# Batch 1's second FFN product as seven half products for eight, with the copies and sums of the half products placed directly behind them

## The chip, the cores and the metric

One core of a Trainium2 chip runs the whole program. The metric is the device time of one execution in microseconds; several executions are timed and the median is taken. TensorE multiplies matrices into PSUM, VectorE and ScalarE read PSUM and SBUF, GpSimd (POOL) works in SBUF and issues most of the loads, SyncE (SP) issues the stores.

## The reference

Attention with a few global tokens and a local window, then a feed-forward network on its result.

```python
# B, H, Sl, D = 8, 8, 512, 64; Sg = 32; window = 32
s_g = scale * q_g @ concat(k_g, k_l).T;   out_g = softmax(s_g) @ concat(v_g, v_l)
s_l = scale * concat(q_l @ k_g.T, where(|i - j| <= 32, q_l @ k_l.T, -1e9))
out_l = softmax(s_l) @ concat(v_g, v_l)
x = concat(out_g, out_l, axis=2).transpose(0, 2, 1, 3).reshape(4352, 512)
h = x @ w_in                      # 512 -> 2048
g = h * sigmoid(1.702 * h)        # "gelu" below
out = g @ w_out                   # 2048 -> 512, float32
```

## The kernel before

The eight batches go through one after the other, and the work of three stages overlaps: while batch i does its two FFN products, batch i+1 does its attention and batch i+2 has its operands loaded and turned. The global tokens of all batches are collected (`xG`) and go through the FFN at the end. There is no scheduler: each engine gets its instructions in the order in which the Python text issues them, and the framework places semaphore waits where one engine reads or overwrites what another wrote or still reads. `tc.manual_schedule()` says so at the top.

**Attention of one batch** is two quads of four heads, `a` and `c` (class `Wide`, L500). A quad's methods are the steps that the change places anew: `Tk` and `Tq` (L509, L522) turn k and q with VectorE transposes; `kcopy`, `qcopy` and `ext` (L503, L506, L528) copy parts beside them, on VectorE, ScalarE or POOL as told; `S(rnd)` (L548) is one of two rounds of scores on TensorE into four PSUM banks, `X(rnd)` (L568) their exponentials on ScalarE, `M(rnd)` (L573) the mask, a multiplication on VectorE or POOL; `U` and `Gm` (L578, L592) multiply with v on TensorE; `R` (L460) makes the reciprocal of the sums on VectorE, `XL` (L470) scales two tiles of the result into `xL`; `G` (L473), or `keep_og` and `GG` (L606, L609), do the same for the global tokens, `GG` for both quads at once from copies that ScalarE made. S, X and M of round 1 need the banks of round 0 free. `spair()` (L284) gives the four score banks, `pbank()` (L280) one of four others in turn.

**First FFN product**: 16 pieces `fc` of 128 of the 2048 columns, each four matmuls of 128x512 (`h_mm`, L627), then a gelu on ScalarE into `gT` (`h_act`, L650; `h_step`, L654, does both). From batch 3 on (`h_some`, L1197) two pairs of pieces are split: class `HPair` (L689) computes a 2x2 block product with seven half products for eight (Strassen's way with sums). Its `mm(k)` is half product k; products 3 and 4 add into one pair of PSUM banks `x`, in different column halves, 1 and 6 into `y`. `m3` (L715) is a ScalarE copy of product 3 out of `x`, `z` and `zm` (L718, L721) are VectorE sums of it with the next ones, then come `sub` and `add` and two gelus.

**Second FFN product**: in batches 0 and 1 four tiles of 128 rows, each 16 matmuls of 128x512 (`o_mm`, L736), copied out by ScalarE and stored (`o_out`, L854). From batch 2 on class `Pair` (L787) does two such tiles as seven half products of eight matmuls of 128x256, from sums of gT that VectorE makes (`g_sums`, L766) and sums of w_out (`weight_sums`, L753; sums 1 and 2 overwrite two quarters of w_out itself). Again `m3` (L816) copies product 3 from bank `px` to `zz` on ScalarE; `z` reads product 4's half of `px`, `zm` product 1's half of `py`; products 6 and 7 write `py`, 5 and 2 `px`; `evict` is ScalarE's copy of `px`, `sub` and `add` are VectorE's.

**The order around the change.** Batch 0's second product holds batch 1's attention (L954 to L1012). Batch 1's first product follows (L1013 to L1045) with weight sums 0, 3, 4 and the turning of batch 2's operands on VectorE; its second product is `phase_o1` (L1064), `o_mm` pieces between the steps of batch 2's attention. Batch 2's first product is a plain loop (L1287 to L1307). Then `phase_o(i)` (L1107) and `h_some(i)` alternate. In `h_some` the split pair opens with `p.mm(3, 4)`, `p.m3()`; in front of it on ScalarE stand the eviction and `gelu_table()` of `phase_o`'s end. Loads are issued by POOL: `load` (q and k of a batch), `load_v`, `load_g` (global q and k), each waiting until the load eight places ahead has landed.

Of the kernel before, what the change touches and what calls it, by code (L numbers as in the profile page):

```python
# [20 lines left out]
def kernel(  # L21
# [584 lines left out]
    def keep_og(q, ogs):  # L606
        on_act(ogs[:, q.u], q.st["og"][:, : D + 2])
# [60 lines left out]
    def h_weight_sums(g):  # L668
        w11, w12, w21, w22 = w_h[g]
        for t, x, y, op in zip(wh[g], (w11, w21, w11, w21, w12), (w22, w22, w12, w11, w22),  # L670
                               (ALU.add, ALU.add, ALU.add, ALU.subtract, ALU.subtract)):
            nc.vector.tensor_tensor(t, x, y, op)
# [77 lines left out]
    wsum = [wts.tile([128, FC // 2, HM], BF16, name="wsum%d" % k) if k in (0, 3, 4) else (b12, b21)[k - 1]  # L750
            for k in range(5)]

    def weight_sums(*ks):  # L753
        for k in ks:
            x, y, op = ((b11, b22, ALU.add), (b12, b22, ALU.subtract), (b21, b11, ALU.subtract),
                        (b11, b12, ALU.add), (b21, b22, ALU.add))[k]
            nc.vector.tensor_tensor(wsum[k], x, y, op)

    sums = {}

# [182 lines left out]
    for fc in range(4, FC):  # L943
        h_step(0, fc)
        if fc == 4:
            h_weight_sums(1)
        if fc == 12:
            h_weight_sums(2)
            h_weight_sums(4)

    def osteps(i, *sts):
        for tci, f4 in sts:
            o_mm(i, 4 * tci + f4)
# [10 lines left out]
    a.S(0)  # L964
    a.X(0)
    copy_vg1()
    c.Tk()
    c.Tq()
    c.ext()
    a.M(0)  # L970
    osteps(0, (0, 2), (1, 2))
    o_mm(0, 10, part=(0, 1))
    a.S(1)
# [40 lines left out]
    for kcs in ((0, 1), (2,), (3,)):  # L1014
        for fc in range(4):
            h_mm(1, fc, hps[fc], kcs)
    a.G()
    c.G()
    weight_sums(0, 3, 4)
    nq[2][0].Tk()  # L1020
    nq[2][0].Tq()
    transpose_g(4, 6)
    nq[2][0].ext()
    pt = spair()
    for fc in range(4, 8):
        h_mm(1, fc, bank(pt, (fc - 2) % 4), range(NKC))

    a, c = nq[2]
    for fc in range(FC):
        if fc == 11:  # L1030
            c.Tk(False)
            c.Tq(False)
            c.ext((0, 1, 2))
            c.kcopy(nc.vector.tensor_copy)
            c.ext((3,))
            c.qcopy(nc.vector.tensor_copy)
        if fc < 4:
            h_act(1, fc, hps[fc])
        elif fc in (4, 6):
            f = slice(fc, fc + 2)  # L1040
            gelu(gTs[1][:, f, :], pt[1 - (fc - 4) // 2])
        elif fc >= 8:
            h_step(1, fc)
        if fc == 13:
            a.S(0)  # L1045

    def o_parts(i, *parts):
        for part in parts:
            o_mm(i, part)

    def loads_after(i):
        if i + 2 < B:
            load_v(i + 2)
        if i == 1:
            load_g(8, NQ)
        if i + 3 < B:
            load(i + 3)

    def quads_of(n):
        if n < B and n not in nq:  # L1060
# [3 lines left out]
    def phase_o1():  # L1064
        a, c = nq[2]
        a2, c2 = quads_of(3)
        a2.T()
        transpose_g(6, 8)
        a2.ext()
        a.X(0)  # L1070
        a.M(0)
        loads_after(1)
        o_parts(1, 0, 1, 2, 3, 4)
        a.S(1)
        a.X(1)
        a.M(1)
        o_parts(1, 5, 6, 7)
        c.S(0)
        c.X(0)
        a.UG()  # L1080
        a.R()
        c.M(0)
        o_parts(1, 8)
        c.S(1)
        c.X(1)
        a.XL(0)
        a.XL(1)
        a.G()
        c.M(1)
        o_parts(1, 9, 10, 11)  # L1090
        a2.S(0)
        a2.X(0)
        c.UG()
        loads_after(2)
        c.R()
        a2.M(0)
        c.XL(0)
        c.XL(1)
        o_parts(1, 12)
        a2.S(1)  # L1100
        a2.X(1)
        gelu_table()
        c.G()
        a2.M(1)
        o_parts(1, 13, 14, 15)

    def phase_o(i):  # L1107
        b = i + 1
        a, c = nq[b]
        a2, c2 = quads_of(b + 1)  # L1110
        p0, p1 = Pair(i, 0), Pair(i, 1)
        ogs = att.tile([128, 2, D + 2], F32, name="ogs", bufs=1)
        late = a2 and i > 2
        exp_table()
        a.UG()
        c.S(0)
        a.R()
        g_sums(i, 7, 8, (0,))
        a.XL(0)
        wide = 2 < i < B - 1  # L1120
        g_sums(i, 7, 8, (1,) if wide else (1, 2))
        a.XL(1)
        g_sums(i, 7, 8, (3,))
        p0.mm(3, 4, 1)
        c.X(0)
        p0.m3()
        p0.z()
        if wide:
            g_sums(i, 4, 8, (2,))
# [12 lines left out]
        p0.mm(5, 2)  # L1142
        p0.sub()
        p0.evict()
        p0.mm(7)
        p0.add()
        p0.store()
        if a2:
            c.UG()
            c.R()  # L1150
            keep_og(c, ogs)
            if i + 3 < B:
                load_v(i + 3, chunks=(0, 1))
            a2.S(0)
            a2.X(0)
            a2.M(0, nc.gpsimd)
            if i + 3 < B:
                load_v(i + 3, chunks=(2, 3, 4))
        else:
            pt = spair()  # L1160
            c.U(0, bank(pt, 0))
            c.U(1, bank(pt, 2))
            c.U(2, bank(pt, 3))
            c.Gm(bank(pt, 1))
            c.R()
            keep_og(c, ogs)
        c.XL(0)
        if a2:
            c.XL(1)
            GG(b, ogs)  # L1170
        p1.mm(3, 4)
        p1.m3()
        p1.z()
        if c2:
            c2.Tk(False)
        else:
            c.XL(1)
# [12 lines left out]
        gelu_table()  # L1190
        p1.mm(7)
        p1.add()
        if a2:
            a2.M(1, nc.gpsimd if i + 3 < B else nc.vector)
        p1.store()

    def h_some(i):  # L1197
# [7 lines left out]
        gs = (1, 2) if c else (1,)  # L1205
        fcs = iter([fc for fc in range(2, 8) if fc // 2 not in gs])
        p = HPair(i, *gs)
        p.mm(3, 4)
        p.m3()
        for fc in range(2):  # L1210
            h_act(i, fc, hps[fc])
        if c:
# [40 lines left out]
            h_step(i, 15)  # L1253
            return
        p = HPair(i, 4)
        p.mm(3, 4)
        p.m3()
        g_sums(i, 0, 2, (0, 1))
        p.z()
        p.mm(1, 6)  # L1260
# [20 lines left out]
        g_sums(i, 4, 6, (3,))  # L1281
        g_sums(i, 6, 8, (3,))

    for i in range(1, B):
        if i > 2:
            h_some(i)
        elif i > 1:  # L1287
            for fc in range(FC):
                h_step(i, fc)
                if i == 2 and fc == 0:  # L1290
                    weight_sums(1, 2)
                if i + 1 < B:
                    c = nq[i + 1][1]
                    if fc == 1:
                        c.Tk()
                        c.Tq()
                        c.ext((3,))
                    if fc in (3, 5, 7):
                        c.ext(((3, 5, 7).index(fc),), on_act)
                    if fc == 9 and i + 2 < B:  # L1300
                        a2 = quads_of(i + 2)[0]
                        a2.T()
                        transpose_g(2 * i + 4, 2 * i + 6)
                        a2.ext()
                if fc in (4, 8, 12):
                    g_sums(i, fc // 2 - 2, fc // 2)
                if fc == 13:  # L1307
                    g_sums(i, 6, 7)
        if i == 1:
            phase_o1()  # L1310
        elif i + 1 < B:
            phase_o(i)

    scores.close()
# [85 lines left out]
```

## Time and profile before

| | |
|---|---|
| median of 3 runs | 284.52 us (284.43 to 284.99) |
| the profiled execution | 284.57 us, its span 282.9 us |
| TensorE clock granted | 1.0 throughout |
| VectorE / ScalarE / POOL busy | 226.6 / 187.1 / 109.9 us |

The stages around the change, from the windows of the profile (us of the span; busy time with instructions in brackets for TensorE, its weight loads, VectorE, ScalarE and POOL; then the granted clock, the DMA share and GB/s). In order: batch 1's first product, its second (`phase_o1`), batch 2's first, its second (`phase_o(2)`).

```profile
51.00:66.00 15.00, 14.74 (x93) 6.76 (x90) 12.34 (x32) 8.49 (x15) 10.30 (x16) 1.00 1.16 189
66.00:85.90 19.90, 19.74 (x366) 10.67 (x368) 15.26 (x32) 15.72 (x18) 14.51 (x21) 1.00 1.57 158
85.90:99.63 13.73, 13.62 (x62) 6.07 (x63) 12.71 (x31) 10.60 (x21) 3.95 (x6) 1.00 1.32 161
99.63:117.44 17.81, 17.76 (x394) 15.23 (x395) 16.66 (x37) 11.11 (x16) 7.29 (x7) 1.00 0.34 47
```

A busy TensorE row counts matmuls that overlap in a pipeline; the number of matmuls and the step from one to the next say more than the share.

### The profile page before, as it was taken

The numbers are of one execution on the slowest core, as the hardware profiler recorded it, in microseconds if no ns is written. First come the engines' busy times: TensorE is split into PE (matmuls) and PEld (weight loads), VectorE is DVE, ScalarE is ACT, GpSimd is POOL, SyncE is SP. The second block draws the span as 40 slices with busy tenths as digits, with TensorE's granted clock in tenths as the row PEclk, the third lists the DMA queues.
The fourth block names the chain that finished last, engine by engine and source line by source line (L and its number), as shares of the span: only waits on it lengthen the run. The fifth ranks groups of instructions, "written<-read, shape, count | busy, mean of one in ns | idle before, by whom it ended". The sixth has DMA issues, their size and how long they took to land.

```text
span 282.9 us, 9001 instructions
## 1 busy us (share of the span) xinstructions
PE 274.3 (97%) x3764; PEld 184.5 (65%) x3787; DVE 226.6 (80%) x490; ACT 187.1 (66%) x319; POOL 109.9 (39%) x157
## 2 busy tenths in 40 slices
PE   6899999999999999999999999999999999999994
PEld 6554445544554478756886488757876589558884
DVE  6687367985689898989998899899997898586452
ACT  4848667577778785579756994779648961873331
POOL 8973551764946004970099106930070000000001
PEclk9999999999999999999999999999999999999999
DMA  7999996899999903994089807920023003300223
GB/s 207 162 196 211 204 156 85 142 220 141 166 166 191 154 3 45 110 158 84 6 115 132 148 5 85 103 58 2 22 59 74 2 2 77 74 3 0 59 53 114
DMA packets 59352, 28.24 MB, mean 100 GB/s; under 512 B 47472, under 2 KB 49776, under 8 KB 59312
## 3 DMA queue, kind: packets, MB, share of 16 engines
q0 software_dynamic: 51760, 17.83, 55.7%
q1 hardware_dynamic: 7120, 9.18, 11.9%
q8 instruction: 29, 0.48, 0.7%
q10 hardware_dynamic: 432, 0.66, 0.7%
q14 instruction: 11, 0.09, 0.1%
HBM read 36.31 MB, written 8.91 MB: 160 GB/s over the span
## 4 chain that ended last, share of the span: by engine, by line
PE 93%; DVE 2%; DMA 2%; ACT 1%; issue 1%; SPq 0%; DVEq 0%
PE hp L629 32%; PE px L812 13%; PE op L743 10%; PE py L812 9%; PE x L812 6%; PE s L560 6%; PE s L711 5%; PE ov L586 5%; PE s L629 2%; DMA early<-in_q_l_dram 2%; DVE xL L471 1%; PE og L597 1%; PE s L357 1%; ACT e L388 1%; PE s L340 1%
## 5 line engine op out<-in xcount | busy, mean ns | idle before, releaser
L629 PE MATMUL hp<-xL,w_in_sb 128*128 128x512 bf16 x385 | 88.7, 379 | 0.9 <-DVE xL L471 0.2
L629 PEld LDWEIGHTS <-w_in_sb 128*128 128x128 bf16 x496 | 48.2, 98 | 48.1 <-issue 0.4
L634 ACT ACTIVATE gT<-hp 128x512 bf16<-128x512 f32 x100 | 57.1, 601 | 13.4 <-PE hp L629 13.0
L571 ACT ACTIVATE e<-s 128x1016 bf16<-128x1016 f32 (+1 forms) x56 | 53.2, 1003 | 17.8 <-PE s L560 17.8
L98 POOL DMA_DIRECT2D v<-in_v_l_dram x40 | 31.1, 779 | 62.8 <-PE og L597 52.6
L812 PEld LDWEIGHTS <-gs 128*128 128x128 bf16 x480 | 46.2, 98 | 6.4
L785 DVE TENSOR_TENSOR gs<-gT 128x256 bf16<-128x256 bf16 (+2 forms) x75 | 28.1, 405 | 4.7 <-ACT gT L634 4.7
L576 POOL TENSOR_TENSOR e<-e,mask 128x1760 bf16<-128x1760 bf16 (+1 forms) x7 | 23.1, 3303 | 19.8 <-ACT e L571 19.7
L812 PE MATMUL py<-wsum,gs 128*128 128x256 bf16 x240 | 30.3, 273 | 0.0
L743 PE MATMUL op<-w_out_sb,gT 128*128 128x512 bf16 x122 | 28.8, 380 | 0.5 <-issue 0.3
L845 POOL DMA_DIRECT2D out_dram<-ob x2 | 1.2, 597 | 65.8 <-ACT ob L113 65.6
L576 DVE TENSOR_TENSOR e<-e,mask 128x1712 bf16<-128x1712 bf16 (+1 forms) x21 | 22.1, 1052 | 2.7 <-ACT e L571 2.4
L512 DVE STREAM_TRANSPOSE kT<-rk 128x512 f32<-128x512 f32 x14 | 14.6, 1041 | 12.0 <-DMA rk<-in_k_l_dram 12.0
L743 PEld LDWEIGHTS <-gT 128*128 128x128 bf16 x128 | 11.8, 98 | 13.9
L812 PEld LDWEIGHTS <-gT 128*128 128x128 bf16 x192 | 18.0, 98 | 2.9
L812 PE MATMUL px<-w_out_sb,gT 128*128 128x256 bf16 x160 | 19.2, 273 | 0.0
L812 PE MATMUL px<-w_out_sb,gs 128*128 128x256 bf16 x160 | 19.1, 273 | 0.0
L471 DVE TENSOR_TENSOR xL<-ov,rs 128x512 bf16<-128x512 f32 x27 | 17.9, 685 | 0.7 <-PE ov L438 0.3
L113 ACT ACTIVATE ob<-px 128x512 f32<-128x512 f32 x10 | 6.0, 598 | 17.9 <-DVE zz L834 17.9
L560 PEld LDWEIGHTS <-kT 32*128 32x128 bf16 x672 | 12.5, 93 | 6.8 <-issue 4.9
L634 ACT ACTIVATE gT<-s 128x1024 bf16<-128x1024 f32 (+1 forms) x10 | 9.3, 938 | 11.5 <-DVE ob L725 7.0
L782 DVE TENSOR_TENSOR gs<-gT 128x1024 bf16<-128x1024 bf16 (+3 forms) x21 | 15.9, 760 | 0.0
(181 smaller groups left out, 452.6 us busy)
## 6 DMA issues: line engine op xcount, KB each, us to landing
out_dram<-ob SPq DMA_DIRECT2D x128, 64.0 KB, 2.4
rq<-in_q_l_dram POOLq DMA_DIRECT2D x5, 512.0 KB, 7.3
rk<-in_k_l_dram POOLq DMA_DIRECT2D x5, 512.0 KB, 8.5
v<-in_v_l_dram POOLq DMA_DIRECT2D x24, 96.0 KB, 4.1
w_in_sb<-in_moe_w_in_dram POOLq DMA_DIRECT2D x8, 256.0 KB, 8.9
w_out_sb<-in_moe_w_out_dram POOLq DMA_DIRECT2D x4, 512.0 KB, 10.6
rk<-in_k_l_dram POOLq DMA_DIRECT2D x5, 256.0 KB, 7.9
rq<-in_q_l_dram POOLq DMA_DIRECT2D x5, 256.0 KB, 7.3
```

The lines of the kernel that those rows point to most:

```text
L98: nc.gpsimd.dma_start(out=vt[0:n, hs, c, :D], in_=vs[FIRST[c] : FIRST[c] + n, hs])
L471: nc.vector.tensor_mul(self.x[:, 2 * self.u + h, :], self.st[1 + h], self.st["rs"])
L512: nc.vector.transpose(flat[:, 0:Sl].rearrange("p (r t) -> p t r", t=16), loaded[self.b][0][:, self.u].bitcast(F32))
L560: nc.tensor.matmul(bank(self.ps, j)[:, at : at + n], lhsT=self.k[p, KEYS[c] : KEYS[c] + 128, e], rhs=qs[p, :, :, e], start=(e == 0), stop= ...
L571: nc.scalar.activation(self.E[rnd][:, 2 * i : 2 * i + 2, :n], self.ps[i][:, :, :n], AF.Exp, scale=scale)
L576: eng.tensor_mul(e, e, mask[:, rnd : rnd + 1, :n].to_broadcast([128, 4, n]))
L629: nc.tensor.matmul(hp[:, : width(i)], lhsT=w_in_c[:, fc // 4, kc, fc % 4 // 2, :, fc % 2], rhs=(xL[i] if i < B else xG)[:, kc, :], start=( ...
L634: nc.scalar.activation(out_, in_, AF.Gelu_apprx_sigmoid)
L743: nc.tensor.matmul(op, lhsT=gTs[i][:, fc, tci * 128 : tci * 128 + 128], rhs=w_out_sb[:, fc, :], start=(first and fc == 4 * f4), stop=(fc = ...
L782: nc.vector.tensor_tensor(sums[i][2][:, g, :n], t[:, g, 0, :n], t[:, g, 1, :n], ALU.add)
L785: nc.vector.tensor_tensor(sums[i][k][:, g, : n // 2], x[:, g], y[:, g], op)
L812: nc.tensor.matmul(out_, lhsT=lv[:, g, tt * 128 : tt * 128 + 128], rhs=rv[:, g, :], start=(g == 0 and k in ((1, 3, 4, 6) if self.apart els ...
```

## The change

Batch 1's second product now goes through `Pair` too, in a new `phase_o1` with its own order of half products, scores and copies. The weight sums are made earlier, 0, 3 and 4 in pieces during batch 0's second product, 1 and 2 during batch 1's first. Batch 1's global rows are kept by ScalarE copies. Batch 2's operand copies of quad a go to ScalarE. Batch 2's first product becomes `h_two`, which holds round 1 of batch 3's scores. In `phase_o(2)` the copies for batch 4 go to ScalarE as they did from `phase_o(3)` on. In `h_some`, in both split pairs, `m3` is issued between half products 3 and 4, where it was issued behind 4.

```diff
-    def weight_sums(*ks):
+    def weight_sums(*ks, g=slice(0, FC // 2)):
...
-            nc.vector.tensor_tensor(wsum[k], x, y, op)
+            nc.vector.tensor_tensor(wsum[k][:, g], x[:, g], y[:, g], op)
...
         if fc == 12:
             h_weight_sums(2)
             h_weight_sums(4)
+    weight_sums(0, 3, 4, g=slice(2, 4))
+    weight_sums(0, 3, 4, g=slice(0, 2))
...
     copy_vg1()
+    weight_sums(0, 3, 4, g=slice(4, 6))
...
     a.M(0)
+    weight_sums(0, 3, 4, g=slice(6, 8))
...
-    a.G()
-    c.G()
-    weight_sums(0, 3, 4)
-    nq[2][0].Tk()
-    nq[2][0].Tq()
-    transpose_g(4, 6)
-    nq[2][0].ext()
+    ogs = att.tile([128, 2, D + 2], F32, name="ogs", bufs=1)
+    keep_og(a, ogs)
+    keep_og(c, ogs)
+    weight_sums(1, 2)
+    GG(1, ogs)
...
+        if fc == 3:
+            g_sums(1, 0, 2)
+            a.Tk(False)
+            a.Tq(False)
+            transpose_g(4, 6)
+        if fc == 6:
+            g_sums(1, 2, 4)
+            c.Tk(False)
+            c.Tq(False)
+            c.kcopy(nc.vector.tensor_copy)
+            c.qcopy(nc.vector.tensor_copy)
+            c.ext()
+        if fc == 8:
+            a.kcopy(on_act)
+        if fc == 9:
+            a.qcopy(on_act)
+        if 10 <= fc < 14:
+            a.ext((fc - 10,), on_act)
         if fc == 13:
-            a.S(0)
+            g_sums(1, 4, 7, (0, 1))
```

The new phase and batch 2's first product, the old bodies left out:

```diff
     def phase_o1():
         a, c = nq[2]
         a2, c2 = quads_of(3)
+        p0, p1 = Pair(1, 0), Pair(1, 1)
+        ogs = att.tile([128, 2, D + 2], F32, name="ogs", bufs=1)
+        load_g(8, NQ)
+        load(4)
+        load_v(3, chunks=(0, 1))
+        g_sums(1, 7, 8, (0, 1))
+        p0.mm(3)
+        p0.m3()
+        p0.mm(4)
+        a.S(0)
         a.X(0)
+        p0.z()
+        g_sums(1, 4, 8, (2, 3))
+        p0.mm(1)
+        p0.zm()
+        p0.mm(6, 5)
         a.S(1)
         a.X(1)
+        a2.Tk(False)
+        a.M(0)
+        p0.mm(2)
+        p0.sub()
+        p0.evict()
+        p0.mm(7)
         a.M(1)
         c.S(0)
         c.X(0)
+        p0.add()
+        p0.store()
+        ov = [pbank("ov"), pbank("ov")]
+        p1.mm(3)
+        p1.m3()
+        a.U(0, ov[0])
+        a.U(1, ov[1])
+        a.U(2)
         a.R()
         c.S(1)
         c.X(1)
+        p1.mm(4)
+        a.Gm()
+        keep_og(a, ogs)
+        a2.kcopy(on_act)
+        c.M(0, nc.gpsimd)
+        load_v(3, chunks=(2, 3, 4))
         a.XL(0)
+        p1.z()
         a.XL(1)
+        p1.mm(1)
+        p1.zm()
+        a2.Tq(False)
+        transpose_g(6, 8)
+        a2.qcopy(on_act)
+        a2.ext(copy=on_act)
         c.M(1)
+        p1.mm(6, 5, 2)
+        p1.sub()
+        p1.evict()
+        p1.mm(7)
+        p1.add()
+        p1.store()
         a2.S(0)
+        ov = [pbank(n) for n in ("ov", "og", "ov", "ov")]
+        c.U(0, ov[0])
+        c.U(1, ov[2])
+        c.U(2, ov[3])
+        c.Gm(ov[1])
+        a2.X(0, (0,))
+        keep_og(c, ogs)
+        a2.X(0, (1,))
         c.R()
-        a2.M(0)
+        a2.M(0, nc.gpsimd)
         c.XL(0)
         c.XL(1)
+        return ogs
+
+    def h_two(ogs):
+        a, c = nq[3]
+        a2 = quads_of(4)[0]
+        pool = nc.gpsimd.tensor_copy
+        gTs[2] = moe.tile([128, FC, TB], BF16, name="gT")
+        hps = [pbank("hp") for _ in range(4)]
+        for fc in (0, 1):
+            h_mm(2, fc, hps[fc], (0, 1))
+        a.S(1)
+        a.X(1)
         gelu_table()
+        for fc in (2, 3):
+            h_mm(2, fc, hps[fc], (0, 1))
+        for kc in (2, 3):
+            for fc in range(4):
+                h_mm(2, fc, hps[fc], (kc,))
+        pt = spair()
+        for fc in range(4, 8):
+            h_mm(2, fc, bank(pt, fc - 4), range(NKC))
+        c.Tk(False)
+        c.Tq(False)
+        c.kcopy(pool)
+        c.qcopy(pool)
+        c.ext((3,), pool)
+        load_v(4)
+        load(5)
+        a2.Tk(False)
+        a2.Tq(False)
+        transpose_g(8, 10)
+        GG(2, ogs)
+        a.M(1)
+        for fc in range(4):
+            h_act(2, fc, hps[fc])
+        g_sums(2, 0, 2)
...
     def phase_o(i):
...
-        late = a2 and i > 2
+        late = a2
...
     def h_some(i):
...
         p = HPair(i, *gs)
-        p.mm(3, 4)
+        p.mm(3)
         p.m3()
+        p.mm(4)
...
         p = HPair(i, 4)
-        p.mm(3, 4)
+        p.mm(3)
         p.m3()
+        p.mm(4)
...
-    for i in range(1, B):
...
+    h_two(phase_o1())
+    phase_o(2)
+    for i in range(3, B):
+        h_some(i)
+        if i + 1 < B:
             phase_o(i)
```

More of the change, by code (lines that the diff above doesn't have):

```diff
@@ L1029 @@
     for fc in range(FC):
[L1030 to L1036, printed above, removed]
         if fc < 4:
@@ L1043 @@
             h_step(1, fc)
-        if fc == 13:
-            a.S(0)
[L1047 to L1057, printed above, removed]
+        if fc == 3:
[16 more added lines that the diff above has]
+            a.ext((fc - 10,), on_act)
+        if fc == 13:
+            g_sums(1, 4, 7, (0, 1))
     def quads_of(n):
@@ L1066, in phase_o1 @@
         a2, c2 = quads_of(3)
-        a2.T()
-        transpose_g(6, 8)
-        a2.ext()
-        a.X(0)
-        a.M(0)
-        loads_after(1)
-        o_parts(1, 0, 1, 2, 3, 4)
+        p0, p1 = Pair(1, 0), Pair(1, 1)
[8 more added lines that the diff above has]
+        a.S(0)
+        a.X(0)
+        p0.z()
+        g_sums(1, 4, 8, (2, 3))
@@ L1074, in phase_o1 @@
+        p0.mm(1)
+        p0.zm()
+        p0.mm(6, 5)
         a.S(1)
         a.X(1)
+        a2.Tk(False)
[4 more added lines that the diff above has]
+        p0.mm(7)
         a.M(1)
-        o_parts(1, 5, 6, 7)
         c.S(0)
         c.X(0)
-        a.UG()
+        p0.add()
[6 more added lines that the diff above has]
+        a.U(2)
         a.R()
-        c.M(0)
@@ L1083, in phase_o1 @@
-        o_parts(1, 8)
         c.S(1)
         c.X(1)
+        p1.mm(4)
[4 more added lines that the diff above has]
+        load_v(3, chunks=(2, 3, 4))
         a.XL(0)
+        p1.z()
         a.XL(1)
-        a.G()
-        c.M(1)
-        o_parts(1, 9, 10, 11)
-        a2.S(0)
-        a2.X(0)
-        c.UG()
-        loads_after(2)
+        p1.mm(1)
[3 more added lines that the diff above has]
+        a2.qcopy(on_act)
@@ L1095, in phase_o1 @@
+        a2.ext(copy=on_act)
+        c.M(1)
+        p1.mm(6, 5, 2)
[4 more added lines that the diff above has]
+        p1.store()
+        a2.S(0)
+        ov = [pbank(n) for n in ("ov", "og", "ov", "ov")]
[6 more added lines that the diff above has]
+        a2.X(0, (1,))
         c.R()
-        a2.M(0)
+        a2.M(0, nc.gpsimd)
         c.XL(0)
         c.XL(1)
-        o_parts(1, 12)
@@ L1100, in phase_o1 @@
-        a2.S(1)
-        a2.X(1)
-        gelu_table()
-        c.G()
-        a2.M(1)
-        o_parts(1, 13, 14, 15)
+        return ogs
[9 more added lines that the diff above has]
+        a.X(1)
+        gelu_table()
+        for fc in (2, 3):
[21 more added lines that the diff above has]
+        g_sums(2, 0, 2)
+        for n in range(2):
+            gelu(gTs[2][:, 4 + 2 * n : 6 + 2 * n, :], pt[n])
+        g_sums(2, 2, 4)
+        for fc in range(8, FC):
+            h_step(2, fc)
+            if fc in (9, 10, 12):
+                c.ext(((9, 10, 12).index(fc),), on_act)
+            if fc == 11:
+                g_sums(2, 4, 6)
+            if fc == 13:
+                g_sums(2, 6, 7)
@@ L1282, in h_some @@
         g_sums(i, 6, 8, (3,))
-    for i in range(1, B):
[L1285 to L1311, printed above, removed]
+    h_two(phase_o1())
[3 more added lines that the diff above has]
+        if i + 1 < B:
             phase_o(i)
```

## The prediction

> **What bounds the kernel now.** I read the page first (busy time, chain), then the waits of TensorE, then the timeline where the changed lines stand. All durations are from the one profiled execution: 284.57 us, of which the span is 282.9 and 1.7 lies around it; the median of the runs is 284.52, so a change of the span is carried over one to one.
>
> ```profile
> span 282.9 us, 9001 instructions
> ...
> PE 274.3 (97%) x3764; PEld 184.5 (65%) x3787; DVE 226.6 (80%) x490; ACT 187.1 (66%) x319; POOL 109.9 (39%) x157
> ...
> PE 93%; DVE 2%; DMA 2%; ACT 1%; issue 1%; SPq 0%; DVEq 0%
> ```
>
> TensorE works 97% of the span and holds 93% of the chain that ended last. Its waits, all longer ones of the whole run (engine and line, what was waited for, us, times, longest):
>
> ```profile
> PE s L357 <- DVE q L316: 1.7, 2, 1.5
> PE w L183 <- POOL ones L159: 1.1, 1, 1.1
> PE s L340 <- ACT e L388: 0.4, 1, 0.4
> PE op L743 <- issue: 0.3, 2, 0.2
> PE s L865 <- issue: 0.2, 1, 0.2
> PE s L629 <- DVE sT L462: 0.2, 1, 0.2
> PE hp L629 <- DVE xL L471: 0.2, 1, 0.2
> ```
>
> The chain has the last of these at 53 us; behind it TensorE never waits noticeably. So a wait put in front of TensorE there has no idle time to go into: it adds its whole length. Work taken off TensorE gains its whole length if its feeders keep up.
>
> The place that decides is the start of a split first product, here batch 3's (start, us, engine, line):
>
> ```profile
> 118.36 0.60 ACT L113 ACTIVATE ob<-px 128x512 f32<-128x512 f32 x1 [1.79 <-DVE zz L834]
> ...
> 118.95 0.60 PE L711 MATMUL s<-sT,w_in_sb 128*128 128x256 bf16 x4
> 118.98 1.28 ACT L634 ACT_TABLE_LOAD   x1
> ...
> 119.38 0.60 PE L711 MATMUL s<-xs,w_in_sb 128*128 128x256 bf16 x4
> ...
> 120.27 0.20 ACT L634 ACTIVATE spot<-spot 128x1 f32<-128x1 f32 x1
> 120.38 0.58 ACT L113 ACTIVATE ob<-s 128x512 f32<-128x512 f32 x1
> ...
> 120.99 0.69 DVE L719 TENSOR_TENSOR ob<-ob,s 128x512 f32<-128x512 f32 x1 [0.91 <-ACT ob L113]
> ```
>
> TensorE does half product 3 (operands sT, w_in) at 118.95 and half product 4 (xs, w_in) at 119.38, right behind it. ScalarE copies product 3 only from 120.38 to 120.96: before that it evicts the last tile of the phase, itself held until 118.36 by VectorE, and loads the gelu table. Today nobody on TensorE waits for that copy.
>
> **The change, part by part.**
>
> (1) Fewer products. Batch 1's second product was 64 matmuls of 512 columns; batch 2's first product, the same 64, takes the chain from 85.89 to 99.70, so 13.81 us. Now it is 2 tiles x 7 half products; the chain gives one (eight matmuls of 256) as 0.87: 14 x 0.87 = 12.2. Gain 1.6.
>
> (2) m3 before mm(4) in the split first products (batches 3 to 7, and a second one in 7). The order in which the changed kernel is built has a wait there that the old one lacks: half product 4's first matmul waits for the ScalarE copy of product 3. It writes other columns, but of the same PSUM bank that the copy reads. ScalarE's own order in front of the copy is unchanged (eviction, table load, a dummy gelu, copy), and what holds the eviction (VectorE's sums L685 and L686 ahead of its L834) is unchanged too. So the wait costs from product 4's start today to the copy's end plus the 0.03 that VectorE needs to start on it (120.99 against 120.96). From the timeline at each place: batch 3: 120.99 - 119.38 = 1.6; batch 4: 152.16 - 150.53 = 1.6; batch 5: 183.23 - 181.62 = 1.6; batch 6: 214.75 - 212.73 = 2.0; batch 7: 243.57 - 242.34 = 1.2, and its second 248.47 - 247.32 = 1.15. Sum 9.2. Queued behind it on TensorE are products 4, 1, 6 and the rest of the first product; ScalarE's gelus and VectorE's sums all become due later, so nothing is gained back. Bounds: no gain, since TensorE has no waiting there to lose, and at least the bare copy, if ScalarE stood ready: 4 x (0.17 end of the matmul, 0.03, 0.58, 0.03) + 2 x 0.6 = 4.4; at most these 9.2 plus 1. I take 9.2, since both ends of each subtraction are rows of the same queues.
>
> The row shows no TensorE wait on another half of a bank, so the trace alone cannot say that the wait must be there; the built order does. The Trainium skill (PSUM — Partial Sum Buffer, PSUM bank collisions raise a hardware error) gives the reason: two engines may not be on the same bank and quadrant together, even at disjoint columns, so semaphores guard by bank. By it the sum is the one here; with a guard by columns it would be the second rival's below.
>
> (3) The same inside batch 1's new phase (starting when its first product ends, about 65.3: 65.99 less the 0.6 of a.S(0), which moves behind it). First tile: mm(4) waits for m3: matmul end 0.17, copy 0.39 (L113 128x256), twice 0.05: 0.65. mm(6) now stands behind zm and waits for it, and VectorE has z 0.33 (L824 at 104.32, the next at 104.65), sums of 2048 elements 1.14 (L782, 1.22 busy) and of 1024 some 0.6, then zm 0.41 (L827) between mm(4)'s end and that point: 0.22 + 2.48 = 2.7 (steps from start to start), while TensorE has only a.S(0) 0.67 and mm(1) 0.97: 1.1 of stall. Second tile: mm(6) behind zm again, VectorE free: 0.17 + 0.41 + 0.07 = 0.65; its mm(4) has U, R and S(1) before it and does not wait. c.S(0) comes only mm(2) and mm(7) (1.85) behind a.S(1) and needs the banks that a.X(1) reads (1.89 plus latency): 0.25; in the old order 2.7 of products stood between. a2.S(1), inside the next first product, needs both halves of X(0), with keep_og between them: 0.45. One more change of matmul shape (0.1, as 1.85 against 2 x 0.87). Sum 3.2. Bounds: 1.3 (the two zm and m3 at a bare 0.4) to 7 (every chain here late by a VectorE transpose, mask and sums, 1.04 + 1.05 + 1.6).
>
> (4) What I cost at nothing, with the cover. Weight sums 0, 3, 4 in twelve pieces of 512 (0.37 each, L785's): six lie in VectorE's 6.5 us of waiting for rk before 32.95 (the POOL queue shows those w_out parts landed by 28.3 and 30.7), three before c.Tk (1.9 idle, part landed by 36.4), three behind a.M(0), which moves a.M(1) to 43.6-44.7, its reader a.U(0) starting at 46.0. Uncovered they are 1.1 a group. Weight sums 1, 2 (2.33) move into the 3.46 that the others leave at 54.9. g_sums of batch 1 (two groups of 1.6, then 0.5 + 0.5 and 0.25 + 0.25), with Tk 1.04, Tq 0.7 and copies, end by my addition at 66.6; mm(1), their first reader, starts at about 68.3, so 1.7 us are spare. c.Tk lies among them and waits for its DMA until 62.19, as today. ScalarE gets six copies (0.3 to 0.54) between gelus of 0.6 in steps of 0.86: gelu 14 ends near 65.2, in time. Evictions turn from four of 0.6 into m3 0.39 and one of 0.6 a tile. On POOL, load_g and load(4) go ahead of load_v(3), then come c.M(0) and a2.M(0) at 3.3 each and three copies: c.M(0) can start at 77.7 and ends at 81, its reader c.U(0) comes at 85; load_v(4), now some 8 us later, is read at 130. SP issues the same 16 stores. In phase_o(2) a2's copies go to ScalarE as in phase_o(3): those two phases last 17.81 and 17.78 today, so nothing.
>
> Sum: -1.6 + 9.2 + 3.2 = 10.8 on 284.57: 295.4, and 295.3 on the median. I forecast 295.3; its own range is 292.5 to 298.
>
> **The rivals.**
>
> A. ScalarE gets to the copy at once, so (2) costs only the bare copies, 4.4: 284.5 - 1.6 + 4.4 + 3.2 = 290.5. For it: in batch 7 the gap is already smaller. Against: the table load of 1.28 starts only behind an eviction that VectorE releases, in every batch at the same distance.
>
> B. The other side: the half products run on without the wait for the copies, and seven for eight is all that is left. Then (2) and the m3 and zm terms of (3) fall away: 284.5 - 1.6 + 0.25 + 0.45 + 0.1 = 283.7, faster. It decides once the waits on copies sum to under 0.8 us over six first products and one phase, that is 0.1 each. For it: the columns are disjoint. Against: the built order names the wait at each place, and one bare copy alone is 0.39.
>
> C. VectorE falls behind in batch 1's new phase. Between 51.0 and 85.9 it is busy 12.34 + 15.26 = 27.6 of 34.9 us. Added are g_sums 6, the two tiles' z, zm, sub, add 2 x 2.2 and weight sums 2.3; gone are weight sums 3.5, two masks to POOL 2.1, and copies of some 2: 32.7 of 34.9. With waits inside, a chain may slip by 3.7 in (3): 284.5 + 14.5 = 299. Against: the spare 1.7 and 0.7 above.
>
> **How the numbers follow.** Forecast 0.74, A 0.10, B 0.06, C 0.10. The range is 290.5 to 298: it takes in A's value and the forecast's own range, and leaves out B and most of C. A measurement of this kernel tells 0.2% (0.6 us) from no change. Faster: B, 0.06. Within 0.2%: 0.01, for cases between B and A. Slower: 0.93.
>
> **What would show it.** In the profile after: TensorE waits at L711 released by ScalarE's L113 copy, six times, 1.1 to 2.0 us each, about 9 in all; at L812 waits on L113 and L827 between 65 and 82; busy TensorE time down by 1.6 while its share falls to about 93%. Batch 2's first product would end near 101, against 99.7 today; from there each batch would be 1.6 longer. If L711 shows no waits, (2) is wrong; if they are near 0.8, A holds; if VectorE is the releaser of long waits between 66 and 90, C.

## The result, and the profile after

| | kernel before | changed kernel |
|---|---|---|
| median of 6 runs each, us | 284.36 (284.06 to 284.99) | 296.34 (296.17 to 296.65) |
| ratio, 95% interval | | 1.0421 [1.0407, 1.0434] |
| profiled run, us | 284.57 | 296.17 |
| its span, us | 282.9 | 294.5 |

The change costs 12 us; 295.3 was predicted. Where it costs them is read first from TensorE's share. The page of the changed kernel, with span, busy time of the engines and the chain that ended last:

```profile
span 294.5 us, 9145 instructions
...
PE 276.2 (94%) x3815; PEld 190.2 (65%) x3835; DVE 231.9 (79%) x494; ACT 191.6 (65%) x339; POOL 117.6 (40%) x162
...
PE 12%; ACT 1%; DVE 0%; issue 0%; ACTq 0%
```

TensorE fell from 97% of the span to 94%: it is idle 18.3 us where it was 8.6. The chain can't be set beside that of before: it is followed back only to 250 us here, so its shares add up to 13%. The waits say more. TensorE's longest waits in the changed kernel (engine, tile and line, what was waited for, us in total, times, longest):

```profile
PE s L711 <- ACT ob L113: 8.7, 6, 1.9
PE py L812 <- DVE zz L827: 1.6, 2, 1.1
PE w L183 <- POOL ones L159: 1.1, 1, 1.1
PE px L812 <- ACT zz L113: 0.5, 1, 0.5
```

The third line stood there before. The other three are new, and they are the three kinds that the prediction named: half product 4 of the split first products behind ScalarE's copy (L711, six times), and in batch 1's phase `mm(6)` behind `zm` (L827) and `mm(4)` behind `m3` (L113). Together they are 10.8 us. The waits in batch 1's phase, each on the first matmul of a half product (start, us; in brackets the idle time before it and what ended it):

```profile
66.29 1.03 PE L812 MATMUL px<-w_out_sb,gT 128*128 128x256 bf16 x8 [0.47 <-ACT zz L113]
...
69.97 1.03 PE L812 MATMUL py<-wsum,gs 128*128 128x256 bf16 x8 [1.09 <-DVE zz L827]
...
80.70 1.03 PE L812 MATMUL py<-wsum,gs 128*128 128x256 bf16 x8 [0.51 <-DVE zz L827]
```

The timeline of the changed kernel at batch 3's first split product, the place that the prediction showed of before (start, us, engine, line, operation; in brackets the idle time before it and its releaser):

```profile
120.40 0.60 ACT L113 ACTIVATE ob<-px 128x512 f32<-128x512 f32 x1 [1.81 <-DVE zz L834]
...
120.97 0.60 PE L711 MATMUL s<-sT,w_in_sb 128*128 128x256 bf16 x4
121.02 1.28 ACT L634 ACT_TABLE_LOAD   x1
...
122.31 0.20 ACT L634 ACTIVATE spot<-spot 128x1 f32<-128x1 f32 x1
122.42 0.58 ACT L113 ACTIVATE ob<-s 128x512 f32<-128x512 f32 x1
...
123.05 0.60 PE L711 MATMUL s<-xs,w_in_sb 128*128 128x256 bf16 x4 [1.49 <-ACT ob L113]
```

ScalarE's row is the one of before, 2.04 us later throughout: eviction, table load, dummy gelu, copy. On TensorE half product 4, which used to start 0.43 behind product 3 (119.38 and 118.95), starts 2.08 behind it (123.05 and 120.97), when the copy is done. That is 1.65 more; 1.6 was predicted for this place.

The whole run can be cut at the first matmul that each batch's attention does with its summed weights (`ov<-e,ones`, L586). In the changed kernel two of these rows read:

```profile
101.64 0.55 PE L586 MATMUL ov<-e,ones 128*32 128x128 bf16 x24
...
134.40 0.55 PE L586 MATMUL ov<-e,ones 128*32 128x128 bf16 x24
```

All of them, as lengths of the stretch from one to the next, in us:

| stretch | before | after | difference | predicted |
|---|---|---|---|---|
| up to batch 1's phase | 46.00 | 45.64 | -0.36 | 0 |
| batch 1's phase and batch 2's first product | 53.63 | 56.00 | +2.37 | +1.6 |
| batch 3's split product in it | 31.10 | 32.76 | +1.66 | +1.6 |
| batch 4's | 31.15 | 32.98 | +1.83 | +1.6 |
| batch 5's | 31.09 | 32.73 | +1.64 | +1.6 |
| batch 6's | 31.11 | 33.14 | +2.03 | +2.0 |
| batch 7's two, to the end of the span | 58.82 | 61.25 | +2.43 | +2.35 |

The last five rows are the copy in front of half product 4: 9.6 against 9.2. The second is batch 1's phase. The first is not the work of the change: TensorE is 0.36 us ahead already at the first matmul of batch 0's first product (17.32 against 17.68), where it has done nothing new yet and has only waited less for q at L357 (0.2 against 1.7 in all). The kernels of the experiments that open as the changed one does take 45.5 to 46.5 us for this stretch, and 47.0 in one execution that was slow throughout, at a lower clock.

### The profile page after: what moved, and what is told of

Read it like the earlier page. It is cut to its first block, busy times and chain, and to the rows that moved or that the text cites. A ratio compares the mean times of both kernels' runs of the same rounds, so it can differ in the third digit from the quotient of the medians.

```text
span 294.5 us, 9145 instructions
## 1 busy us (share of the span) xinstructions
PE 276.2 (94%) x3815; PEld 190.2 (65%) x3835; DVE 231.9 (79%) x494; ACT 191.6 (65%) x339; POOL 117.6 (40%) x162
## 5 line engine op out<-in xcount | busy, mean ns | idle before, releaser
L629 PE MATMUL hp<-xL,w_in_sb 128*128 128x512 bf16 x370 | 85.6, 379 | 1.1 <-DVE xL L471 0.2
L812 PEld LDWEIGHTS <-gs 128*128 128x128 bf16 x560 | 53.9, 98 | 9.5 <-issue 2.0
L576 POOL TENSOR_TENSOR e<-e,mask 128x1760 bf16<-128x1760 bf16 (+1 forms) x9 | 29.8, 3313 | 28.2 <-ACT e L571 28.1
L812 PE MATMUL py<-wsum,gs 128*128 128x256 bf16 x288 | 36.6, 273 | 1.7 <-DVE zz L827 1.6
L785 DVE TENSOR_TENSOR gs<-gT 128x256 bf16<-128x256 bf16 (+3 forms) x86 | 32.7, 410 | 6.5 <-ACT gT L634 6.5
L812 PE MATMUL px<-w_out_sb,gT 128*128 128x256 bf16 x192 | 23.4, 273 | 0.5 <-ACT zz L113 0.5
L812 PEld LDWEIGHTS <-gT 128*128 128x128 bf16 x224 | 20.9, 98 | 4.3 <-issue 0.6
L812 PE MATMUL px<-w_out_sb,gs 128*128 128x256 bf16 x192 | 23.1, 273 | 0.0
L113 ACT ACTIVATE ob<-px 128x512 f32<-128x512 f32 x12 | 7.2, 598 | 18.9 <-DVE zz L834 18.9
L100 POOL DMA_DIRECT2D v<-in_v_g_dram x24 | 14.0, 584 | 2.3 <-DMA rq<-in_q_l_dram 1.7
L560 PE MATMUL s<-q,kT 32*128 32x160 bf16 (+1 forms) x448 | 14.9, 246 | 0.0
```

The source lines that it names most:

```text
L100: nc.gpsimd.dma_start(out=vt[96:128, :, c, :D], in_=vg)
L560: nc.tensor.matmul(bank(self.ps, j)[:, at : at + n], lhsT=self.k[p, KEYS[c] : KEYS[c] + 128, e], rhs=qs[p, :, :, e], start=(e == 0), stop= ...
L576: eng.tensor_mul(e, e, mask[:, rnd : rnd + 1, :n].to_broadcast([128, 4, n]))
L629: nc.tensor.matmul(hp[:, : width(i)], lhsT=w_in_c[:, fc // 4, kc, fc % 4 // 2, :, fc % 2], rhs=(xL[i] if i < B else xG)[:, kc, :], start=( ...
L785: nc.vector.tensor_tensor(sums[i][k][:, g, : n // 2], x[:, g], y[:, g], op)
L812: nc.tensor.matmul(out_, lhsT=lv[:, g, tt * 128 : tt * 128 + 128], rhs=rv[:, g, :], start=(g == 0 and k in ((1, 3, 4, 6) if self.apart els ...
```

## The experiments

The ratios are to the kernel before, timed beside each; its median was 284.35, 284.47 and 284.29 in the three groups. "Kernel 2" is the kernel of experiment 2, and so on.

**1. The copy moved alone** (copy_between_alone). The kernel before, and nothing of the change but step (2), in both places:

```diff
-        p.mm(3, 4)
+        p.mm(3)
         p.m3()
+        p.mm(4)
```

> The kernel before, with only the two lines of the split pairs changed: m3 between half products 3 and 4. Theory W: six waits, 9.2 us by the subtraction of rows, up to 9.6 by the stages: 284.4 + 9.2 to 9.6 = 293.6 to 294.0 us. Rival L: a few us at most, since the rest of the change, which would make the engines late, is missing: 285 to 290.

Measured 293.92 us, ratio 1.0333 [1.0315, 1.0352]: 9.6 us for one step moved in two places, with batch 1's product as it was. TensorE's longest wait in that kernel:

```profile
PE s L711 <- ACT ob L113: 8.4, 6, 1.9
```

The idle time is 8.4 and the time lost 9.6. Most of the rest is the end of the last matmul before each wait, which otherwise overlaps the next one: in the rows above, product 4 starts 1.65 later for 1.49 of idle time, and there are six such places.

**2. The copy moved back** (split_pairs_old_order). The changed kernel with step (2) undone, all else kept.

```diff
-        p.mm(3)
+        p.mm(3, 4)
         p.m3()
-        p.mm(4)
```

> The changed kernel, but in the split first products of batches 3 to 7 half product 4 is issued ahead of the copy m3 again, as before the change. Theory W (each wait of half product 4 for the copy adds its whole length to the path): the stages of batches 2 to 7, which became 9.6 us longer, go back, so 296.3 - 9.6 = 286.7 us, and TensorE has no wait at the half products' line. Rival L (the stages are longer because ScalarE and VectorE do more and are late for other reasons, the wait only shows it): well above, 290 or more. Rival S (batch 1's new phase is the larger loss): above 288.

Measured 293.13 us, 1.0308 [1.0289, 1.0328]: not theory W's 286.7, but where rivals L and S had put it. The L711 waits on L113 were gone, yet only 3.2 us came back. The cut by stretches shows where they stayed: 56.00, then 31.10, **37.72**, 31.10, 31.10 and 58.78. Batch 1's phase has the length that it has in the changed kernel, so it is not S. Of the stretches behind it every one has the length of before (58.78 against 58.82 for the last), but for one that is 6.6 longer. So L's general lateness did not hold either. TensorE's longest waits in this kernel:

```profile
PE px L812 <- DVE zz L824: 2.7, 1, 2.7
PE s L711 <- DVE sT L685: 2.0, 1, 2.0
...
PE s L711 <- DVE ob L719: 0.8, 1, 0.8
```

These three are waits on VectorE, each once and all in the long stretch. VectorE's timeline there, with POOL's:

```profile
146.30 3.88 DVE L613 TENSOR_TENSOR xgg<-ogs,rgg 128x128 bf16<-128x128 f32 x1
146.67 3.34 POOL L576 TENSOR_TENSOR e<-e,mask 128x1760 bf16<-128x1760 bf16 x1
...
152.65 4.80 DVE L685 TENSOR_TENSOR sT<-xL 128x512 bf16<-128x512 bf16 x2
...
153.56 3.27 POOL L576 TENSOR_TENSOR e<-e,mask 128x1712 bf16<-128x1712 bf16 x1
```

L613, 0.29 us in every other phase of this run, takes 3.88 and ends at 150.18, just after POOL's mask multiplication (150.01). What stands behind it on VectorE slides by 3.6, so that the pair of L685, 1.55 before, comes to lie beside POOL's second mask and takes 4.80, to 157.45, where the mask ends at 156.83. That gave a new theory: these VectorE instructions stand until POOL's has ended. Two kernels tested it.

**3. A pause on POOL** (pause_before_mask). Kernel 2 with 0.6 us of useless work added:

```diff
+    pause = consts.tile([128, 4], F32)
...
             a2.X(0)
+            if i == 3:
+                for _ in range(4):
+                    nc.gpsimd.memset(pause, 0.0)
             a2.M(0, nc.gpsimd)
```

> split_pairs_old_order with four tiny memsets of 128x4 on POOL ahead of the first mask multiplication of batch 3's phase (i == 3): no work is moved or taken away, POOL's mask starts some 0.4 us later (0.1 each by the small memsets at the kernel's start). Theory P with a race at the start (line 613 began at 146.30 and POOL's mask is recorded from 146.67, so close together that which of the two goes first decides): the VectorE instruction is through before the mask starts, takes 0.29, and the time is 293.1 - 6.6 = 286.5 to 287. Rival V (order on VectorE or ScalarE): unchanged, 293.1. If 0.4 is too little for the race, 293.1 too, with line 613 still at 3.9.

Measured 286.93 us, 1.0096 [1.0082, 1.0110]: work added to an engine, and 6.2 us gained. VectorE and POOL in that stretch (line numbers behind 635 are higher by 1 here):

```profile
145.94 0.29 DVE L613 TENSOR_TENSOR xgg<-ogs,rgg 128x128 bf16<-128x128 f32 x1
...
146.29 0.60 POOL L1241 MEMSET pause<- 128x4 f32 x4
...
146.85 3.32 POOL L576 TENSOR_TENSOR e<-e,mask 128x1760 bf16<-128x1760 bf16 x1
146.90 1.03 DVE L512 STREAM_TRANSPOSE kT<-rk 128x512 f32<-128x512 f32 x1
...
147.78 0.40 DVE L828 TENSOR_TENSOR zz<-zz,py 128x256 f32<-128x256 f32 x1
...
148.71 2.07 DVE L686 TENSOR_TENSOR sT<-xL 128x512 bf16<-128x512 bf16 x2
```

L613 is through before the mask starts. Under the mask the transpose (one input) and L828 (its second input, py, is in PSUM) keep their durations; the pair sT (two inputs in SBUF) is longer again, by 0.5, and ends 0.6 after the mask. The Trainium skill (SBUF — State Buffer, Who interferes with whom) states that a VectorE instruction with two SBUF inputs contends with a GpSimd instruction that reads SBUF, for ports under an exclusive lock, and that the order of issue decides which of the two is blocked. The trace agrees on the hold: 3.88 for 0.29.

The pair's usual 1.55 is such a hold too. A single sum of this shape takes 0.41 in the same stretch (L685's third, `xs`). In the kernel before, the pair lies under the first mask as well, and ends 0.63 after it (116.80 and 116.17):

```profile
112.83 3.34 POOL L576 TENSOR_TENSOR e<-e,mask 128x1760 bf16<-128x1760 bf16 x1
...
115.25 1.55 DVE L685 TENSOR_TENSOR sT<-xL 128x512 bf16<-128x512 bf16 x2
```

In the stretches of batches 3 to 6, before and after, it ends 0.6 to 0.8 behind that mask every time.

What stays open is why L613 was struck there. In kernel 2 the held L613 is recorded 0.37 ahead of the mask; in batch 3's stretch of the same run it is 0.37 ahead too (114.84 and 115.21), and takes 0.29. The recorded starts don't say which of the two came first.

**4. The mask on VectorE** (mask_on_vector_batch3_phase). Kernel 2 with the first of that stretch's two masks off POOL:

```diff
-            a2.M(0, nc.gpsimd)
+            a2.M(0, nc.vector if i == 3 else nc.gpsimd)
```

> split_pairs_old_order with one instruction moved: in batch 3's phase (i == 3) the first mask multiplication goes from POOL to VectorE. Split_pairs_old_order took 293.13 us, of which one stage has 6.6 more than its neighbours (37.72 against 31.1), with a VectorE multiplication of 3.88 us (0.29 elsewhere) under POOL's mask multiplication. Theory P (that VectorE instruction stands until POOL's mask multiplication beside it has ended, and everything behind it slides): without the POOL instruction beside it, line 613 takes 0.29 again, the stage 31.1 plus at most the 1.05 that the mask takes on VectorE, and the time is 293.1 - 6.6 + 0 to 1.0 = 286.5 to 287.6. Rival V (the stage is long because of the order on VectorE or ScalarE, and the long instruction is only a symptom): VectorE has more to do in that stage, not less, so 293 or more.

Measured 290.5 us, 1.0222 [1.0207, 1.0238], between the two: a miss for the number. The first mask's hold was gone (L613 takes 0.29 again), but 3.8 of the 6.6 came back in another form, and the stretch is 34.9. VectorE, TensorE and POOL there:

```profile
148.12 0.29 DVE L613 TENSOR_TENSOR xgg<-ogs,rgg 128x128 bf16<-128x128 f32 x1
...
149.21 1.91 PE L812 MATMUL px<-w_out_sb,gs 128*128 128x256 bf16 x16 [1.43 <-DVE zz L824]
...
149.84 3.24 POOL L576 TENSOR_TENSOR e<-e,mask 128x1712 bf16<-128x1712 bf16 x1
...
150.88 2.97 DVE L685 TENSOR_TENSOR sT<-xL 128x512 bf16<-128x512 bf16 x2
```

The mask on VectorE, put ahead of the sums that TensorE waits for, makes L824 late (1.43). POOL, with one mask less, starts its second at 149.84 instead of 153.56, and now that one lies over L685. By kernels 3 and 4 the 6.6 are the masks' doing, and 286.93 of kernel 3, not 293.13, is the better measure of the changed kernel without step (2): 296.34 - 286.93 = 9.4 for it.

**5. The table load ahead of the eviction** (table_load_ahead). The changed kernel, with one part of the delay taken off the copy's way:

```diff
         p1.sub()
+        gelu_table()
         p1.evict()
-        gelu_table()
```

> The changed kernel, with the load of the gelu table issued ahead of the last eviction of a phase, in the time in which ScalarE waits for VectorE, instead of behind it. Theory W with ScalarE's queue as the length of the wait: the copy then follows product 3 at once, mm(4) waits some 0.85 at 512 elements; batches 3 to 5 gain 0.8 to 1.0 each, batch 6 1.2, batch 7's first pair 0.65, its second nothing: 4.4 together, 291.9 us. If the length were set by VectorE's release of the eviction or by a fixed latency of the guard: 296.3, nothing gained.

Measured 291.97 us, 1.0265 [1.0245, 1.0285]. The load now falls into the time in which ScalarE waits for VectorE anyway, and the wait on the copy is halved:

```profile
PE s L711 <- ACT ob L113: 4.2, 6, 1.0
```

So of the 9.4 that the order costs, 4.4 are the table load in front of the copy, and 5.0 are the copy itself with what is left ahead of it.

**6. What the wait goes by** (own_bank_batch7, banks_apart_one_tile). Two kernels alter where batch 7's two first products (the last two of the six) put their halves. In the first, products 3 and 5 write a PSUM bank in a tile of their own, apart from product 4's, and the copy, sums and gelus that read them follow; in the second, the halves lie in the two banks of one two-bank tile.

```diff
+            self.x3 = pbank("x3")[:, :HT] if self.n == 1 else None
...
-                        nc.tensor.matmul(t[:, u, h * HT : h * HT + HT], lhsT=lv[:, kc], rhs=rv[:, kc, :],
+                        own = self.n == 1 and k in (3, 5)
+                        nc.tensor.matmul(self.x3 if own else t[:, u, h * HT : h * HT + HT], lhsT=lv[:, kc], rhs=rv[:, kc, :],
...
```

> The changed kernel and its order, but in the two split pairs of batch 7 half products 3 and 5 get a PSUM tile of their own; the sum and the gelu that read both halves become two of half size. Theory W with the shared bank as the reason: half product 4 no longer waits for the copy in batch 7, the last stage loses its two waits of 1.1 and 1.0 (2.1 to 2.4 us), 294.0 to 294.3 us; batches 3 to 6 keep theirs. If the order of the instructions alone made the wait: 296.3 or, by the added small instructions, more.

Measured 294.03 us, 1.0340 [1.0319, 1.0362]: 2.3 less than the changed kernel. Its TensorE waits on the copy, and the two products in question:

```profile
PE s L713 <- ACT ob L113: 6.6, 4, 1.9
```

```profile
251.35 0.38 PE L713 MATMUL x<-sT,w_in_sb 128*128 128x256 bf16 x2
251.57 0.38 PE L713 MATMUL s<-xs,w_in_sb 128*128 128x256 bf16 x2
```

Six waits became four, and half product 4 starts 0.22 behind product 3, with no gap, while ScalarE has yet to copy. Two banks of one tile instead:

```diff
+            self.apart = self.n == 1
+            if self.apart:
+                self.x4, self.y4 = (t[:, :, :HT].rearrange("p (u h) t -> p u h t", u=1) for t in (x, y))
...
-                        nc.tensor.matmul(t[:, u, h * HT : h * HT + HT], lhsT=lv[:, kc], rhs=rv[:, kc, :],
+                        nc.tensor.matmul((self.x4 if t is self.x else self.y4)[:, u, h, :], lhsT=lv[:, kc], rhs=rv[:, kc, :],
...
```

> The changed kernel, in batch 7's split pairs half products 3 and 4 write two different banks of one two-bank tile. The built order still has half product 4 wait for the copy. If so on the chip: the two waits of 1.1 and 1.0 us stay and the time stays at 296.3; the guard then goes by tile. If the waits are gone: 294.2.

One run: 296.04 us, span 294.3 against 294.5, so the 2.3 are not gained. The wait is still there, in another bank than the one copied:

```profile
252.65 0.38 PE L714 MATMUL s<-xs,w_in_sb 128*128 128x256 bf16 x2 [1.10 <-ACT ob L113]
```

So the semaphore that is put between the two is not by bank; by these two kernels it goes by the tile as allocated. The Trainium skill's reason (PSUM — Partial Sum Buffer, PSUM bank collisions raise a hardware error), which the prediction cites, asks for a guard by bank and quadrant. The trace does not agree that this is what sets the wait: the guard in this program is wider, with a wait of 1.10 us across two banks.

**7. The sums behind the next half product** (phase_sums_behind_next). The changed kernel, batch 1's phase alone, both tiles:

```diff
-        p0.mm(1)
+        p0.mm(1, 6)
         p0.zm()
-        p0.mm(6, 5)
+        p0.mm(5)
```

> The changed kernel, with the sum zm in batch 1's new phase issued behind half product 6 in both tiles, not ahead of it; the split pairs keep their waits. Theory W: the two waits for zm, 1.1 and 0.5 from end to start (1.2 and 0.6 from issue to issue), go: 296.3 - 1.7 = 294.6 us. If VectorE's queue is the limit in this phase, whatever the order: the wait comes back at half products 5 or 7 and the time stays within 0.5 of 296.3.

The ratio is 1.0360 [1.0342, 1.0379], which is 294.7 us: 1.6 less, where 1.75 was priced.

**8. All of these waits undone** (all_waits_undone). Kernel 2 with edit 7 and with `m3` of batch 1's first tile behind `mm(4)`. Seven half products for eight, and every copy and sum one product later:

```diff
-        p0.mm(3)
+        p0.mm(3, 4)
         p0.m3()
-        p0.mm(4)
```

> The changed kernel with all three undone: m3 behind half product 4 in the split pairs and in the first tile of batch 1's phase, zm behind half product 6 in both tiles. Theory W: 296.3 - 9.6 (split pairs) - 1.7 (zm) - 0.6 (m3) = 284.4 us, level with the kernel before: the 1.6 us of fewer products are there, and what is left of the new phase (scores that wait for exponentials, about 1) eats most of it. Rival: if VectorE is the limit of the new phase, 285.5 or more.

The ratio is 1.0017 [1.0004, 1.0030], 284.8 us in the median: the 12 us are gone, the mask hold of kernel 2 did not come up (L613 and POOL's mask start 0.62 apart), and still the kernel is not ahead of the one before. What is left of TensorE's waits in batch 1's phase and behind it is small:

```profile
70.47 0.27 PE L560 MATMUL s<-qc,kT 32*128 32x108 bf16 x6 [0.25 <-ACT e L571]
...
85.63 0.27 PE L560 MATMUL s<-qc,kT 32*128 32x108 bf16 x6 [0.16 <-ACT e L571]
...
86.28 0.32 PE L560 MATMUL s<-q,kT 32*128 32x160 bf16 x8 [0.17 <-issue]
```

The first two are scores that come while ScalarE's exponentials still read their banks; for the third the profile names no releaser. Two kernels tried to win these back.

**9. Scores one place later** (scores_one_place_later)**, or the last product behind them** (last_product_behind_scores). Kernel 8 with these sets of scores moved:

```diff
-        p0.mm(5)
+        p0.mm(5, 2)
         a.S(1)
         a.X(1)
         a2.Tk(False)
         a.M(0)
-        p0.mm(2)
...
-        a.S(1)
-        a.X(1)
-        gelu_table()
         for fc in (2, 3):
             h_mm(2, fc, hps[fc], (0, 1))
+        a.S(1)
+        a.X(1)
+        gelu_table()
```

> all_waits_undone (284.8 us, 284.47 for the kernel before) with two sets of scores one place later: a.S(1) of batch 1's phase behind the whole half product 2 instead of ahead of it, and the round-1 scores of batch 3 behind the first half of all four inner tiles instead of two. Its trace shows TensorE idle 0.25 us at the former and 0.16 + 0.17 at the latter. If these waits are all that stands between it and the kernel before, 284.8 - 0.6 = 284.2, a ratio of 0.999; if the later exponentials hold up what follows, 284.8 or more.

Measured 285.84 us, 1.0059 [1.0047, 1.0072], worse than kernel 8. The wait of 0.25 is gone and a longer one has come, at the next scores; and where the second move put matmuls of the first product ahead of the scores, they now wait for `xL`:

```profile
74.23 0.53 PE L560 MATMUL s<-q,kT 32*128 32x160 bf16 x14 [0.64 <-ACT e L571]
...
87.71 1.19 PE L629 MATMUL hp<-xL,w_in_sb 128*128 128x512 bf16 x4 [0.71 <-DVE xL L471]
```

And kernel 8 with the last half product of batch 1 moved behind the next scores (`p1.mm(7)`, `add` and `store` behind `a2.S(0)`):

> As the kernel with all three undone, and half product 7 of the second tile is issued behind the scores of batch 3's first round, so that these scores come 0.9 us earlier and their exponentials have more time before round 1 needs the banks. Theory: the 0.4 us that round 1 waits in batch 2's first product goes, 284.0 us, faster than before by 0.4. If that wait only moves to the copy of the global rows: no change against the kernel with all three undone.

Measured 285.5 us, 1.0035 [1.0021, 1.0048]: a miss too. The scores now come before ScalarE has copied their keys:

```profile
PE s L560 <- ACT kT L113: 0.8, 1, 0.8
```

No version that was run beats the kernel before.

## Why the prediction was right, point by point

**(1) Fewer products, -1.6.** Right for the products. In kernel 8 the fourteen half products take 12.84 us by their starts, in the kernel before the same product takes 14.33. The working had 12.2 and 13.81, the latter from a first product without scores between; both were 0.5 to 0.6 short, so the difference holds. So it is -1.5, and this holds the change of matmul shape that (3) had priced apart with 0.1.

**(2) The copy ahead of half product 4, +9.2.** Right in mechanism and size: six waits at L711, 1.0 to 1.9 of idle time each. It measures 9.6 by the stretches, 9.6 done alone, and 9.4 undone. One end of a subtraction reads 243.58 in the trace where the working has 243.57, which changes nothing. The reason given for the guard, the shared bank, is not what sets the wait here (experiment 6); the sum did not depend on it, since products 3 and 4 share the tile as well as the bank.

One thing stands further up this path than the prediction looked. It took VectorE's sums L685 and L686 as what holds the eviction; L685's pair is itself held by POOL's mask. Behind the pair come L686, L834, the eviction, the table load and the copy, so some 0.7 us of the copy's lateness may come from that mask (an estimate: 1.55 less twice 0.41). This is read from the rows shown in experiment 3; no run moved that mask in a kernel with step (2).

**(3) Batch 1's phase, +3.2.** Right for the waits: by the steps from start to start `m3` costs 0.6 (0.65 predicted), `zm` of the first tile 1.3 (1.1) and of the second 0.7 (0.65). `c.S(0)` is 0.2 (0.25), the round-1 scores of batch 3 0.6 (0.45). That is 3.4 together. Of the 2.6 for the copy and the two sums, undoing them took off 286.93 - 284.8 = 2.1. What stands around them was left out. With (1), the stretch should have grown by 1.6, and it grew by 2.37. The difference is mostly in pieces that were not priced: batch 1's a.U and a.Gm apart take 1.21 + 0.45 where they took 1.37 together, and batch 2's first product, cut by scores, takes 14.3 instead of 13.9. These pieces are read from the rows; no run put them together again.

The sum did not come out by errors that cover each other. (2) is 0.4 above its term, (1) and (3) together 0.8, and that is the 1.2 by which the change of the medians, 12.0, exceeds 10.8.

**(4) What was costed at nothing.** Right, as far as waits show: no TensorE wait on the weight sums, on batch 1's g_sums, on the copies moved to ScalarE, nor on a load appeared in the changed kernel. One cover was thinner than it looked: POOL's masks beside VectorE's two-input sums. In the changed kernel it shows as 1.81 for L685's pair instead of 1.54, in batch 4's stretch, the one that took 0.2 more than predicted (in kernel 8, where no half product waits for the copy, the pair takes 1.82 there and the stretch is not longer); in kernel 2, with everything some tenths elsewhere, it cost 6.6.

**The rivals.** A (bare copies, 290.5) did not hold, though kernel 5 shows that its point was well placed: with the table load out of the way the cost fell to 5.0, near its 4.4. B (no waits, 283.7) is excluded by the three lines of waits; and kernel 8, which has no such waits, shows that even its time was too low by some 1. The pieces that (3) left out account for some 0.5 of it. C (VectorE falls behind) is excluded: of TensorE's waits between 66 and 90 VectorE releases the two of `zm` alone.

**The signs named.** The waits were as named. Batch 2's first product ended at 101.6, not near 101; TensorE's share is 94%, named as about 93%. Wrong was the sign that TensorE's busy time would fall by 1.6: it rose from 274.3 to 276.2. In kernel 8, without the waits, it is 274.9, so some 1.3 of the rise goes with the waits, which fits the end of the last matmul before each being counted in full. In kernel 1, with six of the waits and the products of before, it is 275.6. But in kernel 8 too the 1.6 did not show: with more and smaller groups of matmuls, busy time was no measure of the work saved.

## What to carry to other kernels

A half product saved is worth less than 0.9 us here (two gave 1.5), and a copy put in front of the next product into the same PSUM tile costs whatever stands ahead of that copy on its engine, and not only the copy's own 0.6: place the copy behind one more product, or give it a tile of its own. Before a reader is moved up, look at its engine's queue (an eviction that waits, a table load), and move the load to where that engine idles. When undoing a part gives back less than it cost, cut the run into stretches: here one stretch held the whole difference, and it had another cause.

## What the runs showed of the hardware

A VectorE multiplication of 128x128 took 3.88 us in place of 0.29, and a pair of sums 4.80 in place of 1.55, beside mask multiplications on POOL of 3.3 us. The pair's 1.55 is already longer than two single sums of 0.41, and ends 0.6 us after a mask. Instructions with one input in SBUF kept their time beside the same masks (a transpose 1.03, a sum with its second input in PSUM 0.40). Whether it happens hangs on tenths of a microsecond: the same instruction, recorded 0.37 ahead of the mask, was held in one stretch of a run and not in another, and 0.6 us of memsets of no use on POOL took 6.2 us off the kernel.
